# Attention, routing, experts and a dense block in one kernel: the attention stage with scores in eight parts and the order of four engines as issued

## The chip, the cores and the metric

The kernel runs on one core of a Trainium2 chip, as one launch. Times are device microseconds. Three executions took 1525.34, 1525.36 and 1527.59 us, median 1525.36 us.

## The reference

Eight batches with eight heads of 576 rows and 64 columns go through a two-step attention: 32 packed queries per head gather a summary of the head, and the rows of the head then attend to that summary. The result goes through a capacity-limited router, eight experts and a dense block.

```python
def sm_attn(qq, kk, vv):
    s = scale * np.matmul(qq, kk.transpose(0, 1, 3, 2))
    s = s - np.max(s, axis=-1, keepdims=True)
    a = np.exp(s)
    a = a / (np.sum(a, axis=-1, keepdims=True) + 1e-09)
    return np.matmul(a, vv)
p_packed = sm_attn(p, k, v)               # 32 x 64 per head
out = sm_attn(q, p_packed, p_packed)      # 576 x 64 per head
x = out.transpose(0, 2, 1, 3).reshape(4608, 512)
# router: logits x @ w_gate; tokens taken in order of their logits, at most 576 to each of 8 experts
h = np.maximum(x[mask] @ w1[e], 0.0); y[mask] = h @ w2[e]
h = y @ w_in; g = h * np.tanh(softplus(h)); result = g @ w_out
```

Everything is computed in 32-bit floating point, on TensorE either in its slow 32-bit form (attention) or as three products of split operands (experts and dense block).

## The kernel before

The attention works on 16 units; a unit is four heads of one batch. For each unit `u` these steps are issued (class `Attention`):

- `s1_mm` (L112): scores of the packed queries against the keys. Heads lie in pairs on the 128 rows of TensorE, and `pT` holds zeros where a query meets the other head, so that one product of 128 rows by 64 columns serves two heads. Four products of 288 columns make the unit.
- `s1_max`, `s1_exp`: row maximum on VectorE (L118, L119) and the exponential with its sum on ScalarE (L123).
- `s1_turn` (L130), `s1_keep` (L136, L137): five transposes on TensorE and two ScalarE copies to SBUF, tile `AT`.
- `pk_mm` (L145): the weighted sum of the values, 16 products of 128 rows by 32 columns and four of 64 by 32. `pk_keep` (L151 to L154) divides by the sum and spreads the four heads over a 128 by 256 tile `pp` by a mask, on VectorE. `pk_turn` (L161) transposes it in two halves, and `pk_keep2` (L167) makes two VectorE copies to `ppT`.
- `s2_mm` (L174, L178): gate products of 8 columns, and the scores of all rows of `q` against the summary, again four products of 128 rows by 64 columns.
- `s2_turn`, `s2_max`, `s2_sub`, `s2_exp`, `s2_sum`, `s2_div`, `s2_back`: the second softmax. VectorE transposes blocks of 32 (L184), copies the gate values to `Z` (L185), takes maxima (L189), sums (L201 to L203) and transposes back to the tile `a2` (L219); GpSimd subtracts and scales, in three pieces each (L215), the last unit on VectorE (L211); ScalarE takes the exponential (L197).
- `logits` (L226): two products per unit that accumulate the router's logits in one PSUM tile, `LE`.

`all_units` sorts the steps of all units by `u` plus the step's number in the table `PLAN` and issues them in this order. That is only the order of issue: a scheduler then orders each engine's instructions by its own model of when operands and buffers are ready, in `Attention` for all engines. After the attention, TensorE's order is written by hand (`manual_schedule`, class `Turns`).

Buffers: the scores and `AT`'s source share three PSUM buffers (`big`), the products of `pk_mm` and `pk_turn` share one (`sm`), loads of `k`, `q` and `v` have four buffers each and go through SyncE's queue in the order k, v, q of the unit before; the table `rc` for the router is last in that queue. After the last `logits`, `rt.take` copies `LE` (L306), and the router starts from this copy. The 80 products of `x_rows` (L242: attention times summary, copied by ScalarE at L245 and stored) fill TensorE meanwhile; behind the router come the gathers, the experts and the dense block.

Of the kernel before, what the change touches and what calls it, by code (L numbers as in the profile page):

```python
# [49 lines left out]
PLAN = [('s1_mm', 0), ('s1_max', 0.25), ('s1_exp', 1.06), ('s1_turn', 1.1), ('s1_keep', 1.5), ('pk_mm', 1.51),  # L50
        ('pk_keep', 1.7), ('pk_turn', 1.95), ('pk_keep2', 1.96), ('s2_mm', 2.25), ('s2_turn', 2.55),
        ('s2_max', 3.5), ('s2_sub', 3.65), ('s2_exp', 3.8), ('s2_sum', 3.81), ('s2_div', 4.57),
        ('s2_back', 6.15), ('logits', 6.7)]
# [4 lines left out]
class Attention:  # L58
# [6 lines left out]
    def setup(self, long, short, ld, wk, big, sm):  # L65
        nc, a = self.nc, self.a
        self.long, self.ld, self.wk, self.big, self.sm = long, ld, wk, big, sm
        self.pT = short.tile([128, 2 * NU, 64], F32, name="pT")
        self.wg = short.tile([128, 4, NE], F32, name="wg")
        self.mask = short.tile([128, 256], F32, name="mask")  # L70
        self.A = [short.tile([128, S], F32, name=f"A{i}") for i in range(2)]
        self.Z = [short.tile([128, 56], F32, name=f"Z{i}") for i in range(6)]
        nc.sync.dma_start(self.pT[:, 0:2], a["pT"][:, 0:2])
# [8 lines left out]
        nc.sync.dma_start(self.pT[:, 2:8], a["pT"][:, 2:8])  # L82
        nc.sync.dma_start(self.mask, a["mask"])
# [4 lines left out]
        nc.sync.dma_start(self.pT[:, 8:], a["pT"][:, 8:])  # L88
        for u in range(2, NU):
            for n, w in ("k", u), ("v", u), ("q", u - 1):  # L90
                self.load(w, n)
        self.load(NU - 1, "q")

    def load(self, u, n):
# [7 lines left out]
        else:  # L102
            t = self.ld.tile([128, 2, S], F32, name=n + "t")
# [45 lines left out]
    def pk_keep(self, u):  # L149
# [3 lines left out]
        pp = self.PP[u] = self.long.tile([128, 256], F32, name=f"pp{u}")  # L153
        nc.vector.scalar_tensor_tensor(pp.rearrange("p (h d) -> p h d", h=4),  # L154
                                       self.st["g2", u][:, None, 0:64].to_broadcast([128, 4, 64]), mx[:, 3:4],
                                       self.mask.rearrange("p (h d) -> p h d", h=4), op0=OP.mult, op1=OP.mult)

    def pk_turn(self, u):
        pt = self.st["pt", u] = self.sm.tile([128, 512], F32, name="sm")
        for j in range(2):  # L160
            self.nc.tensor.transpose(pt[:, 128 * j:128 * j + 128], self.PP[u][:, 128 * j:128 * j + 128], self.ident)  # L161

    def pk_keep2(self, u):
        nc, pt = self.nc, self.st["pt", u]
        ppT = self.st["ppT", u] = self.wk.tile([128, 2, 64], F32, name="ppT")
        for j in range(2):
            nc.vector.tensor_copy(ppT[:, j, :], pt[:, 192 * j:192 * j + 64])  # L167

    def s2_mm(self, u):
# [3 lines left out]
        for j in range(2):  # L173
            nc.tensor.matmul(s2[64 * j:64 * j + 64, 1, 288:288 + NE], ppT[:, j, :], self.wg[:, 2 * (u % 2) + j, :],  # L174
                             start=True, stop=True)
        for n in range(2):
            for j in range(2):
                nc.tensor.matmul(s2[64 * j:64 * j + 64, n, 0:288], ppT[:, j, :],  # L178
                                 st["q", u][:, j, 288 * n:288 * n + 288], start=True, stop=True)

    def s2_turn(self, u):
# [3 lines left out]
        nc.vector.tensor_copy(self.Z[u % 6][:, 24:32], s2[:, 1, 288:288 + NE])  # L185
# [639 lines left out]
def fused_kernel(ctx: ExitStack, tc: tile.TileContext, a: dict, out: bass.AP):  # L825
# [25 lines left out]
    att.all_units()  # L851
# [85 lines left out]
def _layouts(inp):  # L937
# [8 lines left out]
    pb = np.zeros((2, D, 2 * NU, 2, 32), np.float32)  # L946
    pr = p.reshape(2 * NU, 2, 32, D)
    for h in range(2):
        pb[h, :, :, h, :] = pr[:, h].transpose(2, 0, 1)
    r["pT"] = pb.reshape(128, 2 * NU, 64)  # L950
    r["wg"] = inp["moe_w_gate"].reshape(4, 128, NE).transpose(1, 0, 2)
# [39 lines left out]
```

## Time and profile before

| what | us |
|---|---|
| median of three runs | 1525.36 |
| the profiled execution | 1521.4 |
| its span | 1519.4 |
| first score product / last logits product begin | 5.27 / 131.69 |
| copy of the logits begins | 132.56 |
| first expert product begins | 188.66 |

Over the whole span PE is busy for 95%, PEld for 78%, DVE for 55%, ACT for 51% and POOL for 12%. These are means over stages with different limits: from 188.66 us to the end PE is busy nearly always, and before that it is not. The stage that the diff touches is the first one, up to 132.56 us.

### The profile page before, as it was taken

How to read it: one execution, taken by the hardware profiler on the slowest of the kernel's cores; microseconds unless marked ns; L12 is line 12 of the kernel's file. 1: busy time of each engine (PE TensorE's matmuls, PEld its weight loads, DVE VectorE, ACT ScalarE, POOL GpSimd, SP SyncE). 2: the span in 40 equal slices, each digit the busy share in tenths (PEclk: the TensorE clock that was granted, in tenths of full speed). 3: DMA queues.
4: the chain of work that ended last, by engine and by line, in shares of the span. 5: the costliest groups of instructions: out<-in, count | busy, mean ns of one | idle time of the engine just before them, and what ended most of it. 6: DMA issues, size and time to landing. Idle time of an engine off the chain costs nothing.

```text
span 1519.4 us, 22513 instructions
## 1 busy us (share of the span) xinstructions
PE 1436.2 (95%) x9009; PEld 1183.9 (78%) x9009; DVE 838.5 (55%) x1779; ACT 781.7 (51%) x966; POOL 183.2 (12%) x269
## 2 busy tenths in 40 slices
PE   6878699999999999999999999999999999999997
PEld 3335478888889899999788888888888888888885
DVE  4775588777778677543344454544445444454443
ACT  2333444433435344444656566565665656666564
POOL 2441301011010103032601010100101010010101
PEclk9999899999999999999999999999999999999999
DMA  9843636363645548452410020201002020100000
GB/s 339 304 143 126 223 131 220 120 217 127 216 141 190 171 143 307 158 179 93 158 56 28 0 83 1 83 0 56 28 1 83 1 76 7 56 28 0 28 0 28
DMA packets 66840, 165.36 MB, mean 109 GB/s; under 512 B 8880, under 2 KB 21808, under 8 KB 66736
## 3 DMA queue, kind: packets, MB, share of 16 engines
q1 hardware_dynamic: 60656, 144.00, 27.9%
q0 software_dynamic: 6080, 19.93, 3.8%
q8 instruction: 71, 1.16, 0.3%
q14 instruction: 33, 0.27, 0.1%
HBM read 117.76 MB, written 46.14 MB: 108 GB/s over the span
## 4 chain that ended last, share of the span: by engine, by line
issue 49%; PE 24%; DVE 5%; DMA 4%; POOL 3%; ACT 2%; SPq 0%; POOLq 0%; DVEq 0%; ACTq 0%
PE pm L624 18%; PE ph L624 3%; PE po L794 2%; DMA raw<-in_w 2%; POOL out L804 2%; DMA raw<-wd 2%; DVE w L547 1%; POOL w L547 1%; ACT w L540 1%; PE pt L693 1%; DVE h L715 1%; DMA xg<-xd,idx 0%; DVE dbig L585 0%; PE pr L379 0%; DVE xl L696 0%
## 5 line engine op out<-in xcount | busy, mean ns | idle before, releaser
L624 PE MATMUL ph<-y,w 128*128 128x512 f32 x1728 | 414.9, 395 | 0.0
L794 PE MATMUL po<-w,g 128*128 128x512 f32 x1728 | 410.1, 394 | 0.9 <-ACT g L769 0.9
L624 PEld LDWEIGHTS ph<-y,w 128*128 128x128 f32 x1728 | 324.1, 188 | 78.2
L794 PEld LDWEIGHTS po<-w,g 128*128 128x128 f32 x1728 | 324.9, 188 | 75.4 <-ACT g L769 1.7
L769 ACT ACTIVATE u<-u 128x1024 f32<-128x1024 f32 (+1 forms) x219 | 229.4, 1049 | 193.5 <-DVE u L773 183.2
L624 PE MATMUL pm<-h,w 128*128 128x288 f32 x1536 | 235.1, 303 | 1.8 <-DVE h L715 1.6
L624 PE MATMUL pm<-xh,w 128*128 128x288 f32 x1024 | 219.3, 304 | 0.7 <-ACT xh L695 0.7
L624 PEld LDWEIGHTS pm<-h,w 128*128 128x128 f32 x1536 | 209.7, 189 | 9.6 <-issue 3.1
L773 DVE TENSOR_SCALAR u<-ph 128x1024 f32<-128x1024 f32 (+1 forms) x73 | 88.2, 1209 | 200.4 <-PE ph L624 200.4
L769 ACT ACT_TABLE_LOAD x144 | 184.8, 1283 | 2.6
L776 DVE TENSOR_TENSOR u<-ph,u 128x1024 f32<-128x1024 f32 (+1 forms) x73 | 88.2, 1209 | 172.5 <-ACT u L769 172.5
L624 PEld LDWEIGHTS pm<-xh,w 128*128 128x128 f32 x1024 | 169.2, 192 | 8.2 <-issue 4.8
L624 PE MATMUL pm<-xl,w 128*128 128x288 f32 x512 | 156.2, 305 | 0.3 <-DVE xl L696 0.2
L778 DVE TENSOR_TENSOR u<-ph,u 128x1024 f32<-128x1024 f32 (+1 forms) x73 | 88.1, 1208 | 73.3 <-ACT u L769 73.3
L769 ACT ACTIVATE g<-u 128x1024 fp32r<-128x1024 f32 (+1 forms) x73 | 76.4, 1048 | 101.3 <-DVE u L778 93.8
L540 ACT ACTIVATE w<-raw 128x1024 fp32r<-128x1024 f32 x80 | 84.4, 1058 | 80.9 <-DMA raw<-in_w 60.6
L804 POOL DMA_INDIRECT out<-ot,idx_all x36 | 35.0, 971 | 726.8 <-DVE ot L802 721.0
L624 PEld LDWEIGHTS pm<-xl,w 128*128 128x128 f32 x512 | 98.3, 192 | 6.5 <-issue 4.4
L714 ACT ACTIVATE h<-pm 128x288 fp32r<-128x288 f32 x128 | 50.9, 405 | 90.4 <-PE pm L624 89.1
L780 DVE TENSOR_TENSOR g<-u,g 128x1024 fp32r<-128x1024 f32 (+1 forms) x73 | 88.2, 1209 | 2.7 <-ACT g L769 2.7
L683 POOL DMA_INDIRECT xg<-xd,idx x40 | 42.2, 1054 | 367.7 <-PE pr L395 186.8
L715 DVE SCALAR_TENSOR_TENSOR h<-pm,h 128x288 fp32r<-128x288 f32 x128 | 57.0, 451 | 51.2 <-ACT h L714 50.1
(160 smaller groups left out, 1133.5 us busy)
## 6 DMA issues: line engine op xcount, KB each, us to landing
raw<-in_w SPq DMA_DIRECT2D x64, 512.0 KB, 4.7
yd<-y SPq DMA_DIRECT2D x64, 288.0 KB, 3.3
kt<-in_k SPq DMA_DIRECT2D x16, 576.0 KB, 9.5
qt<-in_q SPq DMA_DIRECT2D x16, 576.0 KB, 8.8
vt<-in_v SPq DMA_DIRECT2D x16, 512.0 KB, 7.3
xd<-xt SPq DMA_DIRECT2D x32, 256.0 KB, 2.0
draw<-in_win SPq DMA_DIRECT2D x16, 512.0 KB, 4.3
wd<-dbig SPq DMA_DIRECT2D x32, 256.0 KB, 2.9
```

The costliest lines, as they stand in the source:

```text
L540: self.nc.scalar.activation(w[:, 0].rearrange("p a b -> p (a b)"), raw, AF.Copy)
L624: nc.tensor.matmul(out, l, r, start=i == 0 and m == 0, stop=i == n - 1 and m == 2)
L683: nc.gpsimd.indirect_dma_start(out=xg, out_offset=None, in_=self.xd, in_offset=bass.IndirectOffsetOnAxis(ap=idx[:, j:j + 1], axis=0))
L714: nc.scalar.activation(h[:, 0], ph, AF.Relu)
L715: nc.vector.scalar_tensor_tensor(h[:, 1], ph, 0.0, h[:, 0].bitcast(F32), op0=OP.max, op1=OP.subtract)
L769: op = nc.scalar.activation(*args, **kw)
L773: for step in (lambda p: V.tensor_scalar(u[:, p], ph[:, p], 20.0, None, op0=OP.min), lambda p: A(u[:, p], u[:, p], AF.Exp), lambda p: A(u[ ...
L776: lambda p: V.tensor_tensor(u[:, p], ph[:, p], u[:, p], op=OP.max),
L778: lambda p: V.tensor_mul(u[:, p], ph[:, p], u[:, p]),
L780: lambda p: V.tensor_sub(gt[:, 1, p], u[:, p], gt[:, 0, p].bitcast(F32))):
L794: self.nc.tensor.matmul(self.po[m], gt[:, p, i, 128 * m:128 * m + 128], self.cw[8 + f // 2][:, q, f % 2], start=f == 0 and p == q == 0, st ...
L804: st = nc.gpsimd.indirect_dma_start(out=self.out, out_offset=bass.IndirectOffsetOnAxis(ap=self.idx_all[:, c:c + 1], axis=0), in_=ot, in_of ...
```

## The change

- Scores (`s1_mm`, `s2_mm`) go through a new helper `per_head`: eight products per unit, each for one head and one half of the columns, of 64 rows by 32 columns. The upper half of the columns lies on rows 64 to 127 of `k` and `q`, the host lays the data out so, and the two halves write two PSUM banks. `pT` has no zeros any more, and the gate products become four of 64 rows by 32 columns.
- The division after `pk_mm` moves from VectorE (with the mask, 256 columns) to ScalarE, which writes the 64 columns twice (`gg`, 128 columns). One transpose replaces two, one ScalarE copy of 128 columns replaces two VectorE copies (`ppT`), and the copy of the gate values to `Z` goes to ScalarE. A new step `pk_rows` writes `pp` with four ScalarE copies of 32 by 64 into tiles that GpSimd sets to zero at the start. The mask and its load are gone.
- `PLAN` has new numbers, and `all_units` runs under `manual_schedule` for PE, DVE, ACT and POOL, so that each of the four runs the steps in the order in which they are issued.

```diff
+PLAN = [('s1_mm', 0.22), ('s1_max', 0.42), ('s1_exp', 0.6), ('s1_turn', 0.8), ('s1_keep', 1.0), ('pk_mm', 1.4),
...
+        self.pT = short.tile([128, 4 * NU, 32], F32, name="pT")
+        self.wg = short.tile([64, H, NE], F32, name="wg")
...
+        for u in range(NU):
+            self.PP[u] = long.tile([128, 256], F32, name=f"pp{u}")
+            nc.gpsimd.memset(self.PP[u], 0.0)
...
-        for n in range(2):
-            for j in range(2):
-                self.nc.tensor.matmul(s1[64 * j:64 * j + 64, n, 0:288], self.pT[:, 2 * u + j, :],
-                                      st["k", u][:, j, 288 * n:288 * n + 288], start=True, stop=True)
+        self.per_head(s1, self.pT[:, 4 * u:4 * u + 4], st["k", u])
+
+    def per_head(self, out, w, x):
+
+        for h in range(4):
+            for n in range(2):
+                p = slice(64 * n, 64 * n + 64)
+                self.nc.tensor.matmul(out[32 * h:32 * h + 32, n, 0:288], w[p, h], x[p, h], start=True, stop=True,
+                                      skip_group_check=True)
...
-        nc.vector.scalar_tensor_tensor(pp.rearrange("p (h d) -> p h d", h=4),
-                                       self.st["g2", u][:, None, 0:64].to_broadcast([128, 4, 64]), mx[:, 3:4],
-                                       self.mask.rearrange("p (h d) -> p h d", h=4), op0=OP.mult, op1=OP.mult)
+        gg = self.st["gg", u] = self.wk.tile([128, 2, 64], F32, name="gg")
+        nc.scalar.activation(gg, self.st["g2", u][:, None, 0:64].to_broadcast([128, 2, 64]), AF.Copy, scale=mx[:, 3:4])
...
-        for j in range(2):
-            self.nc.tensor.transpose(pt[:, 128 * j:128 * j + 128], self.PP[u][:, 128 * j:128 * j + 128], self.ident)
+        self.nc.tensor.transpose(pt[:, 0:128], self.st["gg", u].rearrange("p n d -> p (n d)"), self.ident)
...
-        for j in range(2):
-            nc.vector.tensor_copy(ppT[:, j, :], pt[:, 192 * j:192 * j + 64])
+        self.nc.scalar.activation(ppT.rearrange("p h k -> p (h k)"), self.st["pt", u][:, 0:128], AF.Copy)
+
+    def pk_rows(self, u):
+        pp = self.PP[u]
+        for h in range(4):
+            p = slice(32 * h, 32 * h + 32)
+            self.nc.scalar.activation(pp[p, 64 * h:64 * h + 64], self.st["gg", u][p, 0], AF.Copy)
...
+        for h in range(4):
+            nc.tensor.matmul(s2[32 * h:32 * h + 32, 0, 288:288 + NE], ppT[0:64, h], self.wg[:, 4 * (u % 2) + h, :],
+                             start=True, stop=True, skip_group_check=True)
+        self.per_head(s2, ppT, st["q", u])
...
-        nc.vector.tensor_copy(self.Z[u % 6][:, 24:32], s2[:, 1, 288:288 + NE])
+        nc.scalar.activation(self.Z[u % 6][:, 24:32], s2[:, 0, 288:288 + NE], AF.Copy)
...
-    att.all_units()
+    E = mybir.EngineType
+    with tc.manual_schedule(engines={E.PE, E.DVE, E.Activation, E.Pool}):
+        att.all_units()
```

What this does to the order of the engines is shown at three places in the middle of the stage. On TensorE before, one unit's turn through the steps; the names are `big` and `sm` for the PSUM tiles, `pp_`, `a_` and `Z_` for tiles of single units, and `x4` counts products of one shape in a row:

```order
L161 MATMUL sm<-ident,pp_1110 128x128 x2
L112 MATMUL big<-kt,pT 64x288 x4
L130 MATMUL big<-ident,A_106 128x128 x4
L130 MATMUL big<-ident,A_106 64x128
L174 MATMUL big<-wg,ppT 64x8 x2
L178 MATMUL big<-qt,ppT 64x288 x4
L145 MATMUL sm<-vt,AT 32x64 x16
L145 MATMUL sm<-ve,AT 32x64 x4
L226 MATMUL LE<-a_9_1284,Z_111 32x384
L226 MATMUL LE<-a_9_1284,Z_111 32x192
L226 MATMUL LE<-a_10_1354,Z_112 32x192
L226 MATMUL LE<-a_10_1354,Z_112 32x384
```

and now, the same stretch of one unit (`gg` is the divided product of `pk_mm`, L119 is the helper `per_head`):

```order
L165 MATMUL sm<-ident,gg 128x128
L137 MATMUL big<-ident,A_106 128x128 x4
L137 MATMUL big<-ident,A_106 64x128
L182 MATMUL big<-wg,ppT 32x8 x4
L119 MATMUL big<-qt,ppT 32x288 x8
L119 MATMUL big<-kt,pT 32x288 x8
L152 MATMUL sm<-vt,AT 32x64 x16
L152 MATMUL sm<-ve,AT 32x64 x4
L231 MATMUL LE<-a_9_1420,Z_110 32x384
L231 MATMUL LE<-a_9_1420,Z_110 32x192
```

Before, the two score products stood apart, with the transposes between the first of them and the second, and the logits came for two units at a time. Now the second scores of a unit (`qt`) are followed at once by the first scores of the unit two after it (`kt`), and every unit has one logits pair behind `pk_mm`. The transposes of `A_106` stand right ahead of the gate products, which wait for `ppT`.

On ScalarE before, two units:

```order
L136 ACTIVATE AT<-big 128x512
L137 ACTIVATE AT<-big 64x128
L123 ACTIVATE A_107,mx<-big,mx 128x576
L197 ACTIVATE w<-w 128x576
L136 ACTIVATE AT<-big 128x512
L137 ACTIVATE AT<-big 64x128
L123 ACTIVATE A_106,mx<-big,mx 128x576
L197 ACTIVATE w<-w 128x576
```

and now, one unit:

```order
L161 ACTIVATE gg<-sm,mx 128x128
L130 ACTIVATE A_106,mx<-big,mx 128x576
L190 ACTIVATE Z_112<-big 128x8
L143 ACTIVATE AT<-big 128x512
L144 ACTIVATE AT<-big 64x128
L169 ACTIVATE ppT<-sm 128x128
L202 ACTIVATE w<-w 128x576
L175 ACTIVATE pp_150<-gg 32x64 x4
```

Four instructions per unit have become eleven: the division `gg` stands ahead of the first exponential, `ppT` behind the copies `AT`, and the four copies to `pp_` behind the second exponential.

On VectorE before, one unit:

```order
L118 TENSOR_REDUCE mx<-big 128x1
L201 TENSOR_REDUCE r<-w 128x18
L119 TENSOR_SCALAR mx<-mx 128x1
L202 TENSOR_SCALAR r<-r 128x18
L203 RECIPROCAL r<-r 128x18
L184 STREAM_TRANSPOSE w<-big 128x576
L185 COPY Z_112<-big 128x8
L154 SCALAR_TENSOR_TENSOR pp_1110<-sm,mx,mask 128x256
L189 TENSOR_REDUCE r<-w 128x18
L167 COPY ppT<-sm 128x64 x2
L151 TENSOR_SCALAR mx<-mx 128x1
L219 STREAM_TRANSPOSE a_9_1284<-w 128x576
```

and now:

```order
L125 TENSOR_REDUCE mx<-big 128x1
L126 TENSOR_SCALAR mx<-mx 128x1
L158 TENSOR_SCALAR mx<-mx 128x1
L159 RECIPROCAL mx<-mx 128x1
L189 STREAM_TRANSPOSE w<-big 128x576
L194 TENSOR_REDUCE r<-w 128x18
L206 TENSOR_REDUCE r<-w 128x18
L207 TENSOR_SCALAR r<-r 128x18
L208 RECIPROCAL r<-r 128x18
L224 STREAM_TRANSPOSE a_9_1420<-w 128x576
```

Three groups of VectorE work are gone (`pp_`, `ppT`, `Z`), and the steps of the second softmax stand in a fixed sequence behind the two small steps at L158 and L159. On GpSimd the four casts that wait for `rc` stood behind piece 79 of the 90 pieces before and stand behind piece 69 now. Behind the last `logits` the order of all five queues is what it was.

## Rows read from the trace of the kernel before

**Rows 1.** Busy time by stretch: length, each engine's busy us, PEclk, DMA share, GB/s

```profile
18.69:104.55 85.86, 70.03 (x916) 34.85 (x916) 59.81 (x173) 27.66 (x64) 34.42 (x72) 0.94 0.77 283
104.55:132.53 27.98, 23.52 (x190) 12.52 (x189) 16.46 (x43) 8.90 (x17) 9.47 (x23) 0.88 0.15 52
...
188.66:1519.40 1330.74, 1292.25 (x7531) 1106.06 (x7531) 727.54 (x1417) 715.83 (x837) 123.42 (x142) 0.99 0.27 92
```

**Rows 2.** The same view, five microseconds in the early attention

```profile
40.00:45.00 5.00, 3.40 (x56) 1.73 (x57) 4.96 (x16) 2.15 (x5) 2.50 (x6) 1.00 1.02 376
```

**Rows 3.** PE timeline: start us, length, instruction; first scores of units 2 and 15, last logits

```profile
18.69 2.19 PE L112 MATMUL big<-kt,pT 128*64 128x288 f32 x8 [0.68 <-DMA kt<-in_k]
...
104.55 1.19 PE L112 MATMUL big<-kt,pT 128*64 128x288 f32 x8
...
131.69 0.84 PE L226 MATMUL LE<-a,Z 128*32 128x192 f32 x4
```

**Rows 4.** DVE timeline: copy of the logits, behind the last product

```profile
132.56 0.55 DVE L306 COPY le<-LE 96x384 f32<-96x384 f32 x1 [2.94 <-PE LE L226]
```

**Rows 5.** PE timeline, one unit at full clock

```profile
99.28 1.19 PE L112 MATMUL big<-kt,pT 128*64 128x288 f32 x8
100.40 0.77 PE L130 MATMUL big<-ident,A 128*128 128x128 f32 x5
101.10 0.29 PE L174 MATMUL big<-wg,ppT 128*64 128x8 f32 x4
101.24 1.17 PE L178 MATMUL big<-qt,ppT 128*64 128x288 f32 x8
102.34 0.65 PE L145 MATMUL sm<-vt,AT 128*32 128x64 f32 x32
102.92 0.32 PE L145 MATMUL sm<-ve,AT 64*32 64x64 f32 x8
```

**Rows 6.** PE timeline, products of `x_rows` on the full array

```profile
140.44 2.14 PE L242 MATMUL px<-pp,a 128*128 128x256 f32 x8
142.51 0.34 PE L379 MATMUL pr<-ge,oh 128*32 128x124 f16 x9
```

**Rows 7.** ACT timeline: first exponential, its sum, the two copies to `AT`

```profile
108.96 0.74 ACT L123 ACTIVATE A<-big,mx 128x576 f32<-128x576 f32 x1 [1.31 <-DVE mx L119]
109.60 0.19 ACT L123 ACTIVATION_READ_ACCUMULATOR A<-big,mx 128x1 f32 x1
110.65 0.60 ACT L136 ACTIVATE AT<-big 128x512 f32<-128x512 f32 x1 [0.86 <-PE big L130]
111.14 0.26 ACT L137 ACTIVATE AT<-big 64x128 f32<-64x128 f32 x1
```

**Rows 8.** PE timeline: the transposes behind that exponential

```profile
109.85 0.77 PE L130 MATMUL big<-ident,A 128*128 128x128 f32 x5 [1.34 <-ACT A L123]
```

**Rows 9.** DVE timeline: maximum, its scaling; eps and reciprocal of the sum

```profile
7.49 0.76 DVE L118 TENSOR_REDUCE mx<-big 128x1 f32<-128x576 f32 x1 [1.72 <-PE big L112]
8.28 0.15 DVE L119 TENSOR_SCALAR mx<-mx 128x1 f32<-128x1 f32 x1
...
37.35 0.14 DVE L151 TENSOR_SCALAR mx<-mx 128x1 f32<-128x1 f32 x1
37.53 0.16 DVE L152 RECIPROCAL mx<-mx 128x1 f32<-128x1 f32 x1
```

**Rows 10.** DVE timeline: sum, scaling, transposition of unit 15

```profile
126.75 0.75 DVE L201 TENSOR_REDUCE r<-w 128x18 f32<-128x576 f32 x1 [0.17 <-ACT w L197]
...
128.05 0.76 DVE L211 TENSOR_TENSOR w<-w,r 128x576 f32<-128x576 f32 x1
128.85 0.78 DVE L219 STREAM_TRANSPOSE a<-w 128x576 f32<-128x576 f32 x1
```

**Rows 11.** Busy time by stretch, at a low granted clock

```profile
56.31:59.72 3.41, 3.32 (x13) 1.30 (x13) 1.74 (x7) 0.68 (x1) 1.44 (x3) 0.52 0.89 352
```

**Rows 12.** PE timeline: the wait ahead of that stretch

```profile
55.64 1.01 PE L226 MATMUL LE<-a,Z 128*32 128x384 f32 x4 [2.03 <-DVE a L219]
```

More of the change, by code (lines that the diff above doesn't have):

```diff
@@ L46, in wait @@
     return WAITS[n][min(k, 3)]
[L50 to L53, printed above, removed]
+PLAN = [('s1_mm', 0.22), ('s1_max', 0.42), ('s1_exp', 0.6), ('s1_turn', 0.8), ('s1_keep', 1.0), ('pk_mm', 1.4),
+        ('pk_keep', 1.58), ('pk_turn', 1.74), ('pk_keep2', 2.01), ('s2_mm', 2.1), ('pk_rows', 2.55), ('s2_turn', 2.72),
+        ('s2_max', 2.87), ('s2_sub', 3.03), ('s2_exp', 3.35), ('s2_sum', 4.09), ('s2_div', 4.33),
+        ('s2_back', 5.3), ('logits', 5.47)]
 TINY = float(np.uint32(0x380FFFFF).view(np.float32))
@@ L67, in setup @@
         self.long, self.ld, self.wk, self.big, self.sm = long, ld, wk, big, sm
-        self.pT = short.tile([128, 2 * NU, 64], F32, name="pT")
-        self.wg = short.tile([128, 4, NE], F32, name="wg")
-        self.mask = short.tile([128, 256], F32, name="mask")
+        self.pT = short.tile([128, 4 * NU, 32], F32, name="pT")
+        self.wg = short.tile([64, H, NE], F32, name="wg")
         self.A = [short.tile([128, S], F32, name=f"A{i}") for i in range(2)]
         self.Z = [short.tile([128, 56], F32, name=f"Z{i}") for i in range(6)]
-        nc.sync.dma_start(self.pT[:, 0:2], a["pT"][:, 0:2])
+        nc.sync.dma_start(self.pT[:, 0:4], a["pT"][:, 0:4])
         self.load(0, "k")
@@ L80, in setup @@
             nc.gpsimd.memset(t, 0.0)
+        for u in range(NU):
+            self.PP[u] = long.tile([128, 256], F32, name=f"pp{u}")
+            nc.gpsimd.memset(self.PP[u], 0.0)
         self.load(0, "v")
-        nc.sync.dma_start(self.pT[:, 2:8], a["pT"][:, 2:8])
-        nc.sync.dma_start(self.mask, a["mask"])
+        nc.sync.dma_start(self.pT[:, 4:16], a["pT"][:, 4:16])
         self.load(1, "k")
@@ L87, in setup @@
         self.load(1, "v")
-        nc.sync.dma_start(self.pT[:, 8:], a["pT"][:, 8:])
+        nc.sync.dma_start(self.pT[:, 16:], a["pT"][:, 16:])
         for u in range(2, NU):
@@ L102, in load @@
         else:
-            t = self.ld.tile([128, 2, S], F32, name=n + "t")
+            t = self.ld.tile([128, 4, S // 2], F32, name=n + "t")
         self.nc.sync.dma_start(t, self.a[n][u])
@@ L172, in s2_mm @@
         s2 = st["s2", u] = self.big.tile([128, 2, 512], F32, name="big")
[L173 to L179, printed above, removed]
+        for h in range(4):
+            nc.tensor.matmul(s2[32 * h:32 * h + 32, 0, 288:288 + NE], ppT[0:64, h], self.wg[:, 4 * (u % 2) + h, :],
+                             start=True, stop=True, skip_group_check=True)
+        self.per_head(s2, ppT, st["q", u])
     def s2_turn(self, u):
@@ L941, in _layouts @@
     for n, t in (("k", k), ("q", q)):
-        r[n] = t.reshape(B, 2, 2, 2, S, D).transpose(0, 1, 3, 5, 2, 4).reshape(NU, 128, 2, S)
+        r[n] = t.reshape(B, 2, 4, 2, S // 2, D).transpose(0, 1, 3, 5, 2, 4).reshape(NU, 128, 4, S // 2)
     vp = v.reshape(B, 2, 4, S, D).transpose(0, 1, 3, 2, 4).reshape(NU, S, 256)
@@ L945, in _layouts @@
     r["ve"] = vp[:, 512:].reshape(B, 2, 64, 256).transpose(0, 2, 1, 3)
[L946 to L951, printed above, removed]
+    pr = p.reshape(4 * NU, 32, D).transpose(2, 0, 1)
+    r["pT"] = np.concatenate([pr, pr])
+    r["wg"] = inp["moe_w_gate"].reshape(H, D, NE).transpose(1, 0, 2)
     r["w1"] = inp["moe_w1"].reshape(NE, 4, 128, 4, 2, 128).transpose(0, 3, 2, 4, 1, 5).reshape(NE, 4, 128, 1024)
@@ L961, in _constants @@
 def _constants():
-    mask = np.zeros((128, 256), np.float32)
-    for h in range(4):
-        mask[32 * h:32 * h + 32, 64 * h:64 * h + 64] = 1
     rc = np.zeros((128, 210), np.float32)
@@ L974, in _constants @@
     rc[:8, 209] = 2.0 ** (NE - 1 - P[:8])
-    return dict(ident=np.eye(128, dtype=np.float32), mask=mask, rc=rc)
+    return dict(ident=np.eye(128, dtype=np.float32), rc=rc)
 def kernel(**inputs):
```

4 lines of the change are left out of this document (1 added, 3 removed).

## The prediction

> **What bounds the kernel now.** I read the busy time by stretch first. From 188.66 us to the end PE is busy for 1292.25 of 1330.74 us at a granted clock of 0.99, and between units 2 and 15 of the attention it is busy for 70.03 of 85.86 us, with DVE at 59.81, ACT at 27.66 and POOL at 34.42 [rows 1]. So the expert and dense part is TensorE's, while in the attention no engine is full. Second, the TensorE timeline: the first scores of unit 2 begin at 18.69 us, when their load has landed, those of unit 15 at 104.55, and the last logits product at 131.69 [rows 3]. That is 13 units in 85.86 us, 6.60 us each, then 27.98 us up to the copy of the logits; VectorE waits 2.94 us for that last product and starts the copy at 132.56 [rows 4]. The router starts from the copy, and behind it the order of all queues is unchanged. What the attention gains up to this copy should therefore move everything behind it, one for one.
>
> **What bounds a unit now.** DVE has 59.81 us of work in 85.86, but waits on others in between, and so do PE and POOL; a wait of 2.03 us for `a2` on PE shows it [rows 12]. The unit is a ring of waits rather than one full engine, so the new unit must be read as a ring too.
>
> **The new ring, step by step.** The order of the four engines is fixed now. TensorE runs the second scores of a unit and behind them the first scores of the unit two later; VectorE takes the maximum; ScalarE divides (`gg`), then takes the exponential; TensorE transposes; ScalarE copies `AT` twice and then `ppT`; and the next second scores wait for this `ppT`. One turn of this ring is one unit. Each price is from start to start, hand-over included:
>
> - Exponential to transposes: 108.96 to 109.85, 0.89 us, since the transposes wait for the read of the sum as well [rows 7, 8].
> - Transposes to the first `AT` copy: 109.85 to 110.65, 0.80 us [rows 7, 8].
> - `AT` to its second part: 0.49. The first takes 0.60, so neighbours on ScalarE overlap by 0.11; the second takes 0.26 and so 0.15 until `ppT` starts [rows 7].
> - `ppT`, 128 columns from PSUM like the 0.26 row [rows 7]: 0.26, and 0.06 of hand-over, as from the end of the sum's read at 109.79 to the transposes [rows 8], 0.32.
> - Gate products: 0.14, as 101.10 to 101.24 [rows 5]; four on 32 columns instead of two on 64.
> - Second scores: 0.62 (worked out below).
> - First scores: 0.62, and 0.12 until the maximum starts: a block ends 0.07 after the next begins (1.19 against 1.12) [rows 5], and a hand-over.
> - Maximum to its scaling: 0.79. From the scaling on to the two small steps of the sum about 0.07, the first of them 0.18, the reciprocal 0.16 and hand-over 0.09: 1.29 us together [rows 9].
> - `gg`: 0.31 less the overlap of 0.10, so 0.21. No row has this form; 0.26 is the nearest [rows 7].
>
> Sum: 0.89 + 0.80 + 0.49 + 0.15 + 0.32 + 0.14 + 0.62 + 0.74 + 1.29 + 0.21 = 5.65 us per unit, against 6.60.
>
> **The price of eight parts.** Before, a score takes eight passes (two per product) in 99.28 to 100.40, 1.12 us, 0.14 each for 288 columns [rows 5]. On the full array eight passes of 256 columns take 140.44 to 142.51, 2.07 us, 0.26 each [rows 6], or 0.29 at 288. So two column halves already run side by side. The value products, four column parts at once, take 32 passes of 64 columns in 0.58 us [rows 5], 0.018 each where one at a time would be 0.065: 3.6 side by side. Now sixteen passes stand on eight different parts. If all eight run together, it is two rounds of at most 1.12 / 4 = 0.28, 0.56, and I add 0.06 for eight more passes to be started: 0.62 us. If only four run together, four rounds, 1.12, as now. One after another it would be 16 x 0.28 = 4.5 us. No row has two row halves at work at once. I take 0.62, since column parts keep what they promise in both rows.
>
> [...]
>
> **What lies beside the ring.** DVE loses the masked product, two `ppT` copies and the `Z` copy. What is left outside the ring is a transposition, a maximum, a sum with two small steps and a transposition back, about 4 x 0.75 + 0.5 = 3.5 us [rows 10], and 1.29 within: 4.8 of 5.65. ACT has 0.89 + 0.49 + 0.15 + 0.15 + 0.21 in the ring or beside it, the second exponential 0.6, and the new `Z` copy and four row copies. Those have no row: the read of the sum, 0.19, and the 0.26 copy bound one of them [rows 7], so five cost 0.5 to 1.3 us. The row copies stand ahead of the next `gg`. The second exponential before them waits for DVE's transposition and maximum behind the reciprocal, about 1.45 us, and for three pieces on POOL, about 1.5; it starts some 3.0 us after `gg`, the row copies end at most 1.7 us after that, and the next `gg` is due at 5.65. So they are covered, with about 1 us to spare; without the cover a unit would cost up to 1 us more. POOL sets 16 tiles to zero while it waits for nothing but the first unit; nothing queues on it then. Its casts wait for `rc`, behind `q` of unit 15 in SP's queue, and stand between pieces that need unit 12; that load can be issued once unit 11's second scores are done, a whole unit plus the softmax's start (over 7 us) earlier, so I price it at 0 to 3 us and take 0.
>
> **Loads.** By the shapes of its tiles a unit needs 576 + 576 + 512 + 64 KB, 1.77 MB. The queues moved 376 GB/s with the engines full [rows 2], 4.7 us a unit. The ring is slower, so loads do not decide, but they do set unit 2: its keys land at 18.69 less the mask's 0.35 us, 18.3.
>
> **The tail.** Unit 15's first scores start at 18.3 + 13 x 5.65 = 91.8. The second scores of unit 14 follow 5.65 - 0.74 = 4.9 later, and then VectorE is full to the end: thirteen steps of 576 columns (two transpositions, two maxima, three sums, four back, two scalings on unit 15), with the small steps behind the sums. A sum with its steps takes 126.75 to 128.05, 1.30, the next steps 0.80 and 0.78 [rows 10]; where another unit's work follows, the overlap saves 0.1. So 3 x 1.2 + 10 x 0.75 = 11.1 us. With 0.9 for the second scores ahead, 0.9 for the last logits product behind, and 0.3 for `x_rows` products that stand between the last logits: 13.2. The copy could start at 91.8 + 4.9 + 13.2 = 109.9 instead of 132.56.
>
> **Clock.** In 56.31 to 59.72 us the granted clock is 0.52, the lower level, behind a wait of 2.03 us on PE [rows 11, 12]. A score that takes 1.19 us at full clock took 2.19 at 18.69 us [rows 3, 5]. The mean of 0.94 between units 2 and 15 [rows 1] is about 10 us at the lower level. In the new ring the longest pause of PE is from the end of the transposes to the gates, 0.80 + 0.49 + 0.15 + 0.32 - 0.70 = 1.06 us. About 2.1 of the ring's 5.65 us are TensorE's; 10 us at half speed would give it some 3 us more, none would give nothing. I add 2 us: 112.
>
> **Sum.** 132.56 - 112 = 20.6 us, against the profiled execution's 1521.4 us (span 1519.4 and 2.0 around it): 1500.8. The median of the runs is 1525.36, 4 us above that execution; I take the saving from the median: 1525.4 - 20.6 = 1504.8.
>
> **Rivals.** First, the change does only half of what it says: the two row halves take turns. The scores then cost 1.12 each, the ring 6.65, and the copy starts at 18.3 + 86.5 + 5.9 + 13.7 + 2 = 126.4: 6 us saved, 1519. For it speaks that no row shows two halves at work; against it, that eight different parts hold eight different weights, as the four of the value products do. Chance 0.10.
>
> Second, slower: passes that alternate between the row halves hold each other up so that two run at a time. The place is `per_head`, the price eight rounds of 0.28 = 2.24 us instead of 0.62, and 1.62 x 2 x 14 units = 45 us: 1550. It decides for slower once one score takes over about 1.35 us, more than now. Against it speak the 3.6 parts side by side of [rows 5]. Chance 0.04.
>
> [...] All of the stage 0.04; a third to two thirds of it, about 1515, 0.07. [...]
>
> **How the numbers follow.** Forecast 0.72, from 1497 (no clock loss, loads a little earlier) to 1512; halves that take turns 0.10; part of the stage at the low level 0.07; both slower rivals 0.08; no change, by a wait that I do not see, 0.03. The range 1495 to 1520 holds the forecast, the halves and part of the clock. Two tenths of a per cent, 3 us, is about what a measurement tells from nothing: faster 0.89, the same 0.03, slower 0.08.
>
> **What would show it.** In the changed profile: scores of 16 passes in about 0.6 us; first scores 5.6 to 5.7 us apart, each turn's longest pause of PE ahead of the gate products, ended by `ppT`; VectorE without gaps from unit 14's second transposition on; the logits' copy near 110 us; the experts' first product near 168 us, and from there the old picture. Scores of 1.1 us, a PEclk of 0.5 through the stage, or a gap on VectorE ahead of its second sum would make it wrong, as would a distance from the copy to the experts other than the old 56 us.

## The result and the profile after

The changed kernel takes 1510.39 us (median; its executions took 1507.26 to 1513.36), beside 1525.98 us for the kernel before in the same job: ratio 0.9889, 95% interval 0.9868 to 0.9910. That is 15.6 us less, where 20.6 were forecast; 1510.4 lies in the forecast's range. The profiled execution took 1508.5 us, its span 1506.7.

Line numbers of the changed kernel: L119 is `per_head`, L182 the gates, L137 the transposes, L130 the first exponential, L143 and L144 the `AT` copies, L161 `gg`, L165 its transposition, L169 `ppT`, L175 the row copies, L190 `Z`, L231 the logits, L247 `x_rows`, L311 the copy of the logits.

Busy time by stretch after the change, the same three stretches as in [rows 1], and then two stretches of three turns each (length, then busy us and count of PE, PEld, DVE, ACT, POOL, then PEclk, DMA share, GB/s):

```profile
18.52:95.75 77.23, 55.56 (x1167) 28.07 (x1167) 56.24 (x125) 46.70 (x153) 36.06 (x78) 0.91 0.89 316
95.75:115.64 19.89, 17.65 (x210) 8.49 (x194) 15.38 (x31) 11.20 (x33) 7.96 (x17) 0.92 0.18 60
173.19:1506.70 1333.51, 1293.68 (x7531) 1107.41 (x7531) 726.10 (x1417) 716.11 (x837) 121.97 (x140) 0.99 0.27 92
...
25.12:44.33 19.21, 14.18 (x270) 7.37 (x262) 12.94 (x29) 10.57 (x35) 7.79 (x17) 0.77 1.03 363
49.92:66.67 16.75, 11.78 (x278) 5.85 (x270) 13.58 (x30) 10.97 (x37) 9.01 (x20) 1.00 1.02 370
```

Thirteen turns take 77.23 us instead of 85.86, 5.94 each instead of 6.60. The last two rows show that this is two different things: at full clock three turns take 16.75 us, 5.58 each, and at a mean clock of 0.77 19.21 us, 6.40 each. Behind the attention PE's busy time is what it was (1293.68 against 1292.25).

One turn at full clock, PE and then ACT (start us, length, instruction, and in brackets the idle time ahead of it with what ended it):

```profile
61.09 0.69 PE L119 MATMUL big<-kt,pT 64*32 64x288 f32 x16
61.71 0.65 PE L152 MATMUL sm<-vt,AT 128*32 128x64 f32 x32
...
64.36 0.77 PE L137 MATMUL big<-ident,A 128*128 128x128 f32 x5 [0.39 <-ACT A L130]
66.12 0.21 PE L182 MATMUL big<-wg,ppT 64*32 64x8 f32 x4 [1.00 <-ACT ppT L169]
...
66.67 0.69 PE L119 MATMUL big<-kt,pT 64*32 64x288 f32 x16
```

```profile
63.21 0.37 ACT L161 ACTIVATE gg<-sm,mx 128x128 f32<-128x128 f32 x1 [1.03 <-DVE mx L159]
63.48 0.73 ACT L130 ACTIVATE A<-big,mx 128x576 f32<-128x576 f32 x1
...
65.16 0.60 ACT L143 ACTIVATE AT<-big 128x512 f32<-128x512 f32 x1 [0.79 <-PE big L137]
65.65 0.26 ACT L144 ACTIVATE AT<-big 64x128 f32<-64x128 f32 x1
65.81 0.27 ACT L169 ACTIVATE ppT<-sm 128x128 f32<-128x128 f32 x1
```

Sixteen passes of a score take 0.62 us (61.09 to 61.71), where [rows 5] had 1.12. The ring can be walked in these rows: `ppT` ends, the gates start, and PE's pause of 1.00 us ahead of them is the longest of the turn, as forecast. ScalarE waits 1.03 us for the reciprocal ahead of `gg`: the row copies in front of it are covered.

The first units, on PE:

```profile
25.12 1.25 PE L119 MATMUL big<-kt,pT 64*32 64x288 f32 x16
26.30 1.08 PE L152 MATMUL sm<-vt,AT 128*32 128x64 f32 x32
...
28.95 0.77 PE L137 MATMUL big<-ident,A 128*128 128x128 f32 x5 [0.40 <-ACT A L130]
30.72 0.24 PE L182 MATMUL big<-wg,ppT 64*32 64x8 f32 x4 [1.00 <-ACT ppT L169]
```

Here a score takes 1.18 us from start to start and the value products 1.01, where the full-clock turn above has 0.62 and 0.58, but the transposes of the same turn take 0.77, as at full clock. TensorE changes its level within every one of these turns; the granted clock, third from the end in these rows, is 0.50 in one stretch and 1.00 in the next:

```profile
24.00:27.00 3.00, 2.88 (x68) 1.53 (x72) 0.49 (x1) 1.65 (x6) 0.10 (x1) 0.50 1.04 325
27.50:30.50 3.00, 1.22 (x14) 0.64 (x6) 2.86 (x7) 1.91 (x7) 1.24 (x3) 1.00 1.02 363
```

The turns from unit 2 to unit 5 take 6.60, 6.60, 6.45 and 6.16 us. The series ends in the turn in which logits products first stand behind the value products (40.73 us); e1 tests whether that is why.

The end of the attention, PE and then DVE:

```profile
112.50 0.84 PE L231 MATMUL LE<-a,Z 128*32 128x192 f32 x4
113.27 1.56 PE L247 MATMUL px<-pp,a 128*128 128x256 f32 x6
114.76 0.84 PE L231 MATMUL LE<-a,Z 128*32 128x192 f32 x4
```

```profile
112.48 0.78 DVE L224 STREAM_TRANSPOSE a<-w 128x576 f32<-128x576 f32 x1
115.64 0.55 DVE L311 COPY le<-LE 96x384 f32<-96x384 f32 x1 [2.38 <-PE LE L231]
```

VectorE is done with the last transposition at 113.26, but unit 15's logits start 1.5 us later, because three `x_rows` products (six passes) stand ahead of them on PE. The copy starts at 115.64 instead of 132.56 [rows 4], 16.9 us earlier. The first expert product comes at 173.19 instead of 188.66, 15.5 us earlier: 1.4 us are lost at the first gather, whose landing PE awaits for 7.57 us instead of 6.20. On PE, before and after:

```profile
183.08 1.12 PE L693 MATMUL pt<-ident,xg 128*128 128x128 f32 x4 [6.20 <-DMA xg<-xd,idx]
```

```profile
167.65 1.12 PE L698 MATMUL pt<-ident,xg 128*128 128x128 f32 x4 [7.57 <-DMA xg<-xd,idx]
```

Expert weights are loaded meanwhile in both kernels; whether they delay this gather is not shown. From the first expert product to the end the profiled execution then takes 1333.51 us instead of 1330.74, so that its span is 12.7 us shorter, not 15.5.

### The profile page after: what moved, and what is told of

Read it like the earlier page. It is cut to its first block, busy times and chain, and to the rows that moved or that the text cites. A ratio compares the mean times of both kernels' runs of the same rounds, so it can differ in the third digit from the quotient of the medians.

```text
span 1506.7 us, 23173 instructions
## 1 busy us (share of the span) xinstructions
PE 1419.1 (94%) x9313; PEld 1175.6 (78%) x9313; DVE 831.5 (55%) x1715; ACT 806.1 (54%) x1078; POOL 187.2 (12%) x285
## 4 chain that ended last, share of the span: by engine, by line
issue 47%; PE 29%; DVE 9%; DMA 7%; ACT 4%; POOL 2%; SPq 0%; POOLq 0%; ACTq 0%; DVEq 0%
PE pm L629 17%; DMA raw<-in_w 5%; PE ph L629 3%; PE px L247 2%; PE po L799 2%; DVE w L552 2%; POOL out L809 2%; PE big L119 2%; DMA raw<-wd 1%; ACT w L545 1%; DVE h L720 1%; POOL w L552 1%; PE pt L698 1%; DVE mx L125 1%; PE big L137 1%
```

## The experiments

The theory after the result: the turn is the forecast's ring; the gain comes from the ring's terms; and the forecast missed the level of TensorE in the first units and the `x_rows` products in the tail. The rivals: the order alone, or the operations alone, bring the gain. Totals are told with the ratio to the kernel before in the same job. The copy of the logits and the turn at full clock are read from one profiled execution of each kernel; the turn repeats within it, and the copy also holds what the clock did in that execution.

**e1, TensorE kept busy in the first units.**

```diff
+    def fill(self, u):
+        for t0, n in ((0, 384), (384, 192)):
+            self.nc.tensor.matmul(self.LE[96:128, 0:n], self.Z[u % 6][:, 0:32], self.A[u % 2][:, t0:t0 + n],
+                                  start=True, stop=True, skip_group_check=True)
+
     def pk_turn(self, u):
+        if u < 4:
+            self.fill(u)
```

> The changed kernel with two more products of 32 columns on TensorE (576 columns together, as a unit's logits take, result unused) ahead of the transposition of gg in units 0 to 3, where no logits products stand yet. Theory A (TensorE is too empty in the first units, so its level falls in every turn, and from unit 4 on the logits products end that): granted clock 1.00 between 25 and 45 us instead of 0.66 to 0.90, first scores of unit 5 near 35.5 us instead of 38.17, copy of the logits near 112 instead of 115.64, 3 to 4 us less in all: about 1506.5. Theory B (the low level there comes from the start of the program or of the loads, whatever TensorE does): the two products only lengthen units 0 to 3, first scores of unit 5 at 38 to 40, 0 to 2 us more than the changed kernel's 1510.4.

1504.89 us, ratio 0.9876 (0.9854 to 0.9899). First scores at 18.76, 24.36, 29.93 and 35.51 us: 5.58 each from unit 2 on, as theory A says, with scores of 0.62 us from start to start, so at the upper level. The copy came at 113.24, 2.4 us earlier, where ten more turns of 5.58 and the changed kernel's 19.89 us behind them would put it at 111.2. The 2.4 us are within what the clock changes from execution to execution (first scores of unit 15 at 95.75 us in the changed kernel, at 98.43 and 97.72 in e3 and e4), and the intervals of the totals overlap: the level is shown, its worth in time is not.

**e2, the same products ahead of every unit's gates.** The edit is two such products, reading the next unit's `A`, at the head of `s2_mm` for all units.

> The changed kernel with the same two extra products, but ahead of the gate products of every unit, in the pause of 1.00 us that PE makes there while ScalarE copies AT and ppT. At the full level they take 0.83 us and fit in. Theory A: the clock stays at 1.00 from unit 2 to 15, first scores 5.6 us apart in all 13 units, copy near 111, 4 to 5 us less than the changed kernel: about 1506. Theory B: at the low level they take 1.6 us, overrun the pause by 0.6 in units 2 to 5, and the copy comes 2 us later, 1512.

1502.01 us, ratio 0.9863 (0.9841 to 0.9884). Both theories are half right. Behind 46 us the clock is 1.00 without a break, with nine turns of 5.60 us:

```profile
65.82 0.77 PE L137 MATMUL big<-ident,A 128*128 128x128 f32 x5 [0.39 <-ACT A L130]
66.51 1.16 PE L182 MATMUL LE<-A,Z 128*32 128x384 f32 x4
67.60 0.21 PE L186 MATMUL big<-wg,ppT 64*32 64x8 f32 x4
```

The products took 1.16 us, not 0.83, and just fill the pause. But in units 0 and 1 they came at the lower level, in unit 3 in part, took 2.13, 2.13 and 1.61 us and overran it (unit 2 starts at 20.05, its turn is 7.43), so the copy stood at 115.52, no earlier than before the edit. The lower total came behind the router: the profiled execution took 1325.9 us from the first expert product to the end, the changed kernel's 1333.5.

**e3 and e4, the `x_rows` products behind the last logits.** `e4_px18` also has 18 instead of 20 turns ahead of the router's first count.

```diff
...
         for i in range(5 * B):
-            att.x_rows(i, turns)
+            with tc.issue_after(att.last.ins) if i >= 5 else ExitStack():
+                att.x_rows(i, turns)
```

> The changed kernel, with the three x_rows products that stood between the last two units' logits put behind unit 15's logits. Theory A: the last logits product starts at 113.3 us instead of 114.76, the copy near 114.2 instead of 115.64; but the products stand ahead of the router's first count now, PE waited there only 0.51 us for VectorE, so only about 0.5 us of it arrives behind the router: 1509.9. Rival: the whole 1.4 us arrives, 1509.0, since the router's chain does not wait for PE.

> As the run before, and two turns of x_rows fewer ahead of the router's first count (18 instead of 20), so that what moved behind the logits does not delay it. Theory A: copy near 114.2, first gather near 160.4 instead of 161.83, all of the 1.4 us arrives: 1509.0. Rival: the x_rows that now end later delay the gather, which waits for their stores: no gain over the changed kernel, 1510.4.

1513.16 (ratio 0.9919, 0.9894 to 0.9945) and 1513.32 us (0.9928, 0.9902 to 0.9954): no gain over the change. The copy's wait for PE fell from 2.38 to 0.93 us, and from the first scores of unit 15 to the copy `e3_px` took 17.87 us instead of 19.89, so the products did cost the tail 1.4 us; the other 0.6 is the clock, which in `e3_px` fell ahead of this stretch (0.66 at 90 to 95 us). But from the copy to the first gather it then took 47.11 us instead of 46.19: 0.9 of the 1.4 us were given back in the router, as theory A says. In `e4_px18` the rival won, since the gather then waited for the stores of `x_rows`:

```profile
164.45 1.16 POOL L688 DMA_INDIRECT xg<-xd,idx  x1 [1.48 <-DMA xd<-xt]
```

Up to unit 13 both run the changed kernel's order, so they show two more executions of its first units, and those are worse: unit 15's first scores start at 98.43 and 97.72 us, not 95.75. On PE in `e3_px`:

```profile
25.91 1.25 PE L119 MATMUL big<-kt,pT 64*32 64x288 f32 x16
...
29.75 1.33 PE L137 MATMUL big<-ident,A 128*128 128x128 f32 x5 [0.25 <-ACT A L130]
...
33.08 1.25 PE L119 MATMUL big<-kt,pT 64*32 64x288 f32 x16
```

Now the transposes too take 1.33 us: TensorE stayed at the lower level to about 43 us, and the turns of units 2 to 4 took 7.17 us.

**e5, the first scores alone back in four products.** The old layout of `k` and `pT`, and in `s1_mm`:

```diff
...
-        self.per_head(s1, self.pT[:, 4 * u:4 * u + 4], st["k", u])
+        for n in range(2):
+            for j in range(2):
+                self.nc.tensor.matmul(s1[64 * j:64 * j + 64, n, 0:288], self.pT[:, 2 * u + j, :],
+                                      st["k", u][:, j, 288 * n:288 * n + 288], start=True, stop=True)
```

> The changed kernel with the first scores alone taken back to the old four products of 128 rows by 64 columns (the old layout of k and pT); the second scores stay in eight parts. Theory A (the eight parts are worth what they take off the ring): first scores 1.12 us instead of 0.62, a turn at full clock 6.1 us instead of 5.58, 13 turns 6.5 us more, copy of the logits near 122 and first expert product near 179.5, the whole 6 to 7 us slower than the changed kernel's 1510.4: 1517. Rival: the ring is held elsewhere and has room for it, turn 5.6, copy 115 to 116.

1523.90 us, ratio 0.9982 (0.9966 to 0.9998): all but 2 us of the gain is gone. The mechanism is as theory A says, the size of the total is not. At full clock:

```profile
88.68 1.19 PE L114 MATMUL big<-kt,pT 128*64 128x288 f32 x8
89.80 0.65 PE L155 MATMUL sm<-vt,AT 128*32 128x64 f32 x32
...
94.82 1.19 PE L114 MATMUL big<-kt,pT 128*64 128x288 f32 x8
```

The score takes 1.12 us and the turn 6.14 instead of 5.58, 0.55 more. But the clock was 0.50 to 0.69 between 25 and 45 us, with turns of 7.1 to 8.3 us there, and the copy came at 128.22 instead of 122. So the total shows the ring's 0.55 us a turn and, in this profile, a lower clock beside it; that the four products cause the lower clock is not shown.

**e6, the small copies on VectorE again.** `gg` as a `tensor_scalar`, `ppT` and `Z` as `tensor_copy`, in the same place of the order.

> The changed kernel with the division (gg), the copy ppT and the copy Z on VectorE again, in the same place of the order; the row copies stay on ScalarE. VectorE has about 4.8 us of a turn and gets some 0.6 more. Theory A (VectorE would become the full engine or hold ppT back behind its transposition and maximum, which is what the move to ScalarE avoids): turn 5.8 to 6.2 us, copy 118 to 124. Rival: ppT no longer waits behind both AT copies on ScalarE, VectorE fits with 5.4 us, and the turn is 5.4 to 5.6 us: copy 113 to 116, the move to ScalarE was worth nothing.

1504.65 us, ratio 0.9867 (0.9851 to 0.9883). The rival won by more than it claimed: the turn is 5.05 us and the copy comes at 106.36. On DVE:

```profile
63.53 0.77 DVE L189 STREAM_TRANSPOSE w<-big 128x576 f32<-128x576 f32 x1
64.23 0.12 DVE L190 COPY Z<-big 128x8 f32<-128x8 f32 x1
64.34 0.75 DVE L194 TENSOR_REDUCE r<-w 128x18 f32<-128x576 f32 x1
65.01 0.28 DVE L169 COPY ppT<-sm 128x128 f32<-128x128 f32 x1
65.21 0.74 DVE L206 TENSOR_REDUCE r<-w 128x18 f32<-128x576 f32 x1
```

VectorE is now the full engine, busy for 43.25 of 45.44 us in nine turns. `ppT` is finished at 65.29, while on ScalarE it started at 65.81 in a turn whose first scores began 0.24 us later (61.09 against 60.85). So the move of the copies, a part of the change, costs 0.54 us a turn in the order that it was given.

**e7, the new operations without the fixed order.** Only the `manual_schedule` around `all_units` is taken out.

> The changed kernel without the order as issued: the scheduler orders the four engines in the attention by its own model, as before the change; the operations and the table of numbers are the new ones. Theory A (the order is a large part of the gain): a turn of 6.0 to 6.6 us with waits at changing places, copy 121 to 128. Rival: the operations alone bring the gain and the scheduler finds as good an order, turn 5.6, copy 114 to 117.

1536.42 us, ratio 1.0069 (1.0050 to 1.0087), slower than before. From unit 2 to unit 15 a turn takes 7.52 us on average (20.31 to 118.05), more than either theory gave, and the copy comes at 141.43. In eleven of these turns PE waits 1.0 to 2.8 us for the exponential ahead of the transposes, where the fixed order has 0.4.

**e8 and e11, the old operations in a fixed order.** `manual_schedule` around `all_units` in the kernel before; `e8_old_newplan` has the new numbers in `PLAN`, `e11_old_oldplan` the old ones.

> The kernel before, with its old operations (four products, mask, copies on VectorE), in the new table's order as issued on the four engines. By the ring of the prediction with the old prices: two scores at 1.12 instead of 0.62, the masked product and the two ppT copies on VectorE, ppT behind VectorE's transposition and maximum: 6.7 to 7.2 us a turn against 6.60, copy 133 to 140, 0 to 7 us slower than before. Rival: the order alone brings part of the gain, turn 6.2 or less, copy under 129.

> The kernel before, old operations and old table, but in the order as issued on the four engines. It tells whether the new numbers or the mere fact of a fixed order brought the 5.89 us a turn of the run with old operations and new numbers. Theory A (the numbers do it): turn over 6.4 us, copy at 126 or later, 1520 to 1530. Rival: a fixed order alone does it: turn 5.9 to 6.1, copy at 118 to 121, about 1510.

`e8_old_newplan`: 1509.41 us, ratio 0.9901 (0.9880 to 0.9921), turn 5.89, copy at 118.44. `e11_old_oldplan`: 1515.55 us, ratio 0.9937 (0.9914 to 0.9960), turn 5.91, copy at 122.26. The rival won in e8, and in e11 by the turn; e11's copy and total lie between its theories. In `e8_old_newplan` PE runs:

```profile
55.53 1.16 PE L178 MATMUL big<-qt,ppT 128*64 128x288 f32 x7
56.42 1.24 PE L112 MATMUL big<-kt,pT 128*64 128x288 f32 x8
57.59 0.65 PE L145 MATMUL sm<-vt,AT 128*32 128x64 f32 x32
...
61.16 0.35 PE L174 MATMUL big<-wg,ppT 128*64 128x8 f32 x3 [0.62 <-DVE ppT L167]
```

with both scores at about 1.1 us and nothing of the new operations, only 0.3 us a turn behind the change. With the falls of the clock the thirteen turns took 5.80 us on average in `e11_old_oldplan` and 6.01 in `e8_old_newplan`, where the kernel before took 6.60 and the changed one 5.94. So a fixed order, with either table, brings what the mean turn gained, and e8's total (0.9901) cannot be told from the changed kernel's (0.9889).

The rows say where. The kernel before takes logits for two units at a time, and PE waits 2.03 us for the second unit's `a` at 55.64 [rows 12], 70.06, 84.32 and 97.81 us; from unit 6 on its turns alternate between 5.3 to 6.0 and 8.2 to 8.8 us. In `e11_old_oldplan` every turn from unit 6 to unit 15 has one logits pair and no such wait; PE's longest pause in one of them is

```profile
58.22 0.44 PE L161 MATMUL sm<-ident,pp 128*128 128x128 f32 x2 [0.81 <-DVE pp L154]
```

No run takes the pairs apart by themselves. The new numbers bring the copy 3.8 us forward, by the tail (20.8 us from unit 15's first scores to the copy against 28.2).

**e9, `ppT` ahead of the `AT` copies.** One number of the table:

```diff
-... ('pk_keep2', 2.01) ...
+... ('pk_keep2', 1.9) ...
```

> The changed kernel with one number of the table changed, pk_keep2 from 2.01 to 1.9: on ScalarE the copy ppT stands ahead of the two AT copies of the next unit instead of behind them; nothing else moves. Theory A (in the new ring ppT, and with it the gate products, waits for AT copies that it does not need; putting the copies on VectorE gained because of that): PE's pause of 1.00 us ahead of the gates goes, the turn falls from 5.58 to 4.7 to 4.9 us, where VectorE's 4.7 us and the loads' 4.7 us are next; copy of the logits at 103 to 106, 10 us less at the first expert product. Theory B (the gain of the run with the copies on VectorE came from less work on ScalarE): turn 5.5 to 5.6, copy 115 to 116, no gain.

1493.08 us, ratio 0.9804 (0.9781 to 0.9826), all of it below the changed kernel's interval. The turn at full clock is 4.58 us, 5.00 in the mean of thirteen, the copy comes at 101.96 and the first expert product at 158.07, 15.1 us before the changed kernel's. On ACT and on PE:

```profile
51.88 0.28 ACT L169 ACTIVATE ppT<-sm 128x128 f32<-128x128 f32 x1
52.79 0.60 ACT L143 ACTIVATE AT<-big 128x512 f32<-128x512 f32 x1 [0.62 <-PE big L137]
```

```profile
51.99 0.77 PE L137 MATMUL big<-ident,A 128*128 128x128 f32 x5 [0.39 <-ACT A L130]
52.69 0.21 PE L182 MATMUL big<-wg,ppT 64*32 64x8 f32 x4
52.72 0.44 PE L119 MATMUL big<-qt,ppT 64*32 64x288 f32 x2
```

`ppT` runs while PE transposes, and the gates follow the transposes without a pause. That is theory A, by more than it claimed (4.7 to 4.9), and it can explain what e6 gained; theory B (less work on ScalarE) falls, since ScalarE has as much work as in the changed kernel (11.00 us in three turns, 10.97 there). What holds the turn now is VectorE, busy for 13.24 of 13.75 us in three turns, with the loads beside it (DMA share 1.03; a unit's 1.77 MB take 4.7 us at 380 GB/s):

```profile
39.48:53.23 13.75, 11.80 (x279) 5.97 (x271) 13.24 (x31) 11.00 (x37) 8.67 (x19) 1.00 1.03 380
```

**e10, the row copies three times.**

> The changed kernel with each of the four row copies of a unit (pk_rows) done three times, 2.06 us more on ScalarE per unit. In the changed kernel ScalarE waits 1.03 us per turn for the reciprocal ahead of gg. Theory A (the copies are covered up to this wait): turn 5.58 + 2.06 - 1.03 = 6.6 us, copy near 129. Rival: the cover is larger, since gg itself is not on the longest path: turn 5.6 to 5.9, copy under 120.

1522.36 us, ratio 0.9991 (0.9976 to 1.0006). The turn is 6.66 us and the copy comes at 129.16, as theory A says. On ACT the wait ahead of `gg` is gone:

```profile
59.36 3.31 ACT L176 ACTIVATE pp<-gg 32x64 f32<-32x64 f32 x12
62.70 0.37 ACT L161 ACTIVATE gg<-sm,mx 128x128 f32<-128x128 f32 x1
```

So the cover is the 1.03 us that the profile shows: of the 2.06 us added, the 1.03 beyond it should count, and the turn grew by 1.08.

**e12, e9 with the products of e1.**

> The kernel with ppT ahead of the AT copies (1493.1 us, turn 4.58, copy of the logits at 101.96), and with the two extra TensorE products ahead of gg's transposition in units 0 to 3. In its profile the turns up to unit 5 took 6.05, 5.07, 5.34 and 5.07 us. Theory A (the lower level of TensorE costs these 3 us): turns of 4.6 to 4.8 from unit 2 on, copy near 99.5, 1490 to 1491. Rival (the loads hold these turns): no change, or 1 us more, 1493 to 1494.

1497.64 us, ratio 0.9817 (0.9792 to 0.9842), copy at 103.30: no gain over e9. TensorE is at full clock from 17 us to unit 15 (value products 0.65 us), but now the keys are late; from unit 2 to unit 15 PE waits five times for them, 3.3 us in all, as here for unit 4:

```profile
28.61 0.72 PE L119 MATMUL big<-kt,pT 64*32 64x288 f32 x16 [0.59 <-DMA kt<-in_k]
```

The rival was nearer, and e9 stays the fastest version.

## Why the prediction was right, and where its sizes were off

**The ring: right.** Forecast and measured, from start to start at full clock (rows above; the steps on VectorE from the same turn):

| step | forecast | measured |
|---|---|---|
| exponential to transposes | 0.89 | 0.88 |
| transposes to `AT` | 0.80 | 0.80 |
| `AT`, its second part | 0.49 + 0.15 | 0.49 + 0.16 |
| `ppT` to gates | 0.32 | 0.31 |
| gates | 0.14 | 0.04 |
| second scores | 0.62 | 0.51 |
| first scores to maximum | 0.74 | 0.82 |
| maximum to `gg` | 1.29 | 1.30 |
| `gg` to exponential | 0.21 | 0.27 |
| sum | 5.65 | 5.58 |

The sum is closer than its terms: the gates run between the first of the second scores, 0.55 us for both where 0.76 was forecast, and the first scores and `gg` came out longer, so that errors of up to 0.11 us cancel in part.

**The price of eight parts: right.** 0.62 us was forecast for a score and 0.62 is measured for the first scores (0.06 of the forecast had no row), so the rivals of halves that take turns (1.12) and of passes that hold each other up (2.24) are out.

**What lies beside the ring: right.** The row copies were covered with "about 1 us to spare"; the wait is 1.03 us, and e10 shows that it is this wait that covers. GpSimd's casts start at 90.85 us, right behind the piece ahead of them, so taking 0 for the wait on `rc` was right in this execution. VectorE's thirteen steps in the tail took 11.0 us (102.25 to 113.26), 11.1 were forecast.

**The clock: too small.** Two us were added. Thirteen turns at 5.58 are 72.5 us, and they took 77.23: 4.7. The four turns from unit 2 to unit 5 make 3.5 of it, and a fall at 71.5 us most of the rest (turns of 6.04 and 6.15). In `e3_px` and `e4_px18` thirteen turns took 79.7 and 79.0 us, which is 7.2 and 6.5 for the clock. The forecast took a wait of 2.03 us as what lowers the level [rows 11, 12]. The trace of the kernel before does not bear that out: of PE's four waits of this length only the first two (55.64, 70.06 us) were followed by a fall, while behind the other two (84.32, 97.81) the granted clock stayed 1.00. And in the changed kernel's turns from unit 2 to unit 15 it fell although no pause of PE there was over 1.01 us and none was for a DMA, while the full-clock turns behind the first units pause as long (1.00 us). What it depends on stays open beyond what e1 shows, that with more products in the first units the level stayed up there (scores of 0.62 us, turns of 5.58). The rival "part of the stage at the low level" (0.07, about 1515) is so a part of what happened, and in the execution of `e3_px` more than that. Its rows are a score of 1.25 us and transposes of 0.77 in the same turn, three turns in a row.

**The tail: 1.8 us too small.** From unit 15's first scores to the copy 18.1 us were forecast and 19.89 measured. The second scores of unit 14 came 5.65 instead of 4.9 us behind unit 15's first, at a clock of 0.66 (95 to 100 us), and the `x_rows` products ahead of the last logits cost 1.5 instead of 0.3, a term for which the forecast named no row. e3 shows the latter: with these products moved and the clock's fall ahead of the stretch, it took 17.87.

Together: 91.8 became 95.75 (0.2 by a later start, 0.9 back by the shorter ring, 4.7 by the clock) and 112 for the copy became 115.64; 16.9 us instead of 20.6.

**Behind the copy: not one for one.** "Copy to experts 56 us" became 57.55 by the gather's landing, by the forecast's own sign a miss of 1.4 us. What then comes at the end is less exact than its argument assumed: of 16.9 us at the copy 12.7 are left in the span of the profiled pair, while the medians differ by 15.6. How near the total came is therefore partly chance. In all fourteen profiles the program behind the first gather is the same, yet from the first expert product to the end it took from 1325.9 (e2) to 1340.1 us (e6). Part of it goes with the clock in the experts, here in 520 us behind the first expert product, first in `e2_fill_gate`, then in `e6_copies`, which shows 76 products fewer:

```profile
172.85:692.85 520.00, 493.82 (x4096) 458.85 (x4097) 365.80 (x1094) 228.05 (x400) 57.99 (x65) 0.99 0.52 175
```

```profile
162.98:682.98 520.00, 490.52 (x4020) 455.34 (x4021) 362.21 (x1088) 221.38 (x392) 59.14 (x66) 0.97 0.52 174
```

Why e2's executions were short here (1500.8 to 1503.0 in all) and e6's long stays open: the 9 us by which e6's copy leads e2's did not show in the totals.

**What the prediction did not see.** It priced the operations and took the order as given. The runs show the order as the larger part: with the old operations in a fixed order a turn takes 5.9 us at full clock (e8, e11), where the kernel before took 6.60 in the mean, with the new ones 5.58, and with the new ones in the scheduler's order 7.52 in the mean (e7). Of the operations the eight parts gain (0.55 for one score, e5) and the move of the copies to ScalarE loses (0.54, e6), because `ppT` stands behind two `AT` copies there. That place is in the forecast's own sum, as 0.49 + 0.15 of the ring and as PE's longest pause, 1.06 us; it was priced right and not asked whether it had to be there.

## What to carry to other kernels

When a unit is a ring of waits, write the ring down with its start-to-start times, and ask of each link whether it is an operand or only a place in a queue: `ppT` waited for two copies that it does not read, and one number of the table was worth nearly as much as the whole change (15.1 us against 15.5 at the first expert product). Try the order and the operations apart before crediting either. Judge a change in one stage at that stage's last event (here the copy of the logits), since a later stage can vary by nearly as much as the change is worth (14.2 us over these profiles, against 15.6).

## What the runs showed of the hardware that was not expected

- The two row halves of TensorE run side by side, nearly in full: sixteen passes of 288 columns in 64 rows by 32 columns take 0.62 us, 0.31 for a round of eight; eight passes in 128 by 64 take 1.12, 0.28 for a round of two.
- PEclk of a window is not enough. In `e3_px` it reads 1.00 in every window of 5 us up to 55 us, while scores up to 42 us took 1.25 us and transposes 1.33, both at the lower level; the duration of a known product tells the level.
- The same order of instructions ran its first units in two ways: turns of 6.60 us with a change of level in each (the changed kernel), and of 7.17 us at the lower level throughout (e3, e4). With two more products per unit they took 5.58 us (e1).
